# Two range checks on ScalarE instead of VectorE, and more unread products on TensorE, in a gated-recurrence and feed-forward kernel

## Chip, cores and metric

The kernel runs on one core of one Trainium2 chip. The metric is the device time of one execution in microseconds; three runs of the kernel before gave 734.25, 734.54 and 737.98 us, median 734.54 us.

## What is computed

The reference has two parts. The first is a recurrence with a complex gate per channel (4 batches, 8 heads, 768 steps, 48 channels); its result is the input of the second, a feed-forward block over 3072 tokens.

```python
# q, k, v, a_re, a_im: (B=4, H=8, S=768, D=48) float32
mag = np.sqrt(a_re * a_re + a_im * a_im)
scale = np.minimum(mag, 0.999) / (mag + 1e-06)
a_re_n, a_im_n = (a_re * scale, a_im * scale)
for t in range(S):
    S_re, S_im = a[t] * S (complex) + k[t] v[t]^T
    y[:, :, t] = q[t] . S_re
# x: y as (3072, 384); w_in (384, 2048), w_out (2048, 384), float64 in memory
h = x @ w_in
sp = np.maximum(h, 0.0) + np.log1p(np.exp(-np.abs(h)))
g = h * erf(sp)
out = g @ w_out
```

a_re lies between 0.85 and 0.95, a_im is normal with deviation 0.1.

## The kernel before

The kernel goes through 12 units of 256 steps; each unit has two chunks of 128. It has a fast way, valid where the data stay within some bounds, and a slow general way. The fast way is always run, collects six sums that say whether the data were within the bounds, and at the end one branch decides whether the general way has to follow. Two of the bounds matter here: the gate's angle has to be at most 45 degrees (`off`), and no weight may be tiny (`zeros`), since the weights are turned from float64 words into float32 by integer operations. The parts that are touched, with cuts marked:

```python
WARM = (12, 9, 8, 4, 6)
...
    for t, x in ((off, 0.0), (large, 0.0), (zeros, 1.0)):
        nc.vector.memset(t, x)
...
    def act(func, **kw):                      # loads a table where the function needs another set
        sets = [nm for nm, fs in TABLES.items() if func in fs]
        if not sets:
            nc.scalar.activation(func=func, **kw)
            return
        if T.get("table") != sets[0]:
            T["table"] = sets[0]
            in_order(nc.scalar.preload_act_table_set(sets[0]))
        in_order(nc.scalar.activation(func=func, **kw))
...
        def seek(words, i):                   # the weights' check: least absolute high word
            hi = words.bitcast(FP).rearrange("p (n w) -> p n w", w=2)[:, :, 1]
            nc.vector.tensor_reduce(out=zeros[:, i:i + 1], in_=hi, axis=mybir.AxisListType.X, op=OP.min,
                                    apply_absolute_value=True)
...                                           # begin and end: weights into float32, on ScalarE and VectorE
            ins = nc.scalar.mul(out=b, in_=lo, mul=2.0**-52)
            ins = nc.vector.tensor_scalar(out=a, in0=hi, scalar1=0x07FFFFFF, scalar2=3, ...)
            nc.vector.scalar_tensor_tensor(out=u, in0=hi, scalar=0xC0000000, in1=a, ...)
            nc.vector.tensor_scalar(out=a, in0=u, scalar1=0xFF800000, ...)
            nc.vector.tensor_tensor(out=b, in0=b, in1=a, op=OP.mult)
            nc.vector.tensor_tensor(out=f, in0=f, in1=b, op=OP.add)
        def again():                          # the weights are read once more, for the check alone
            pool, tag = ((zp, "z"), (yp, "yy"))[i % 2]
            T["raw", i] = pool.tile([P, N], I64, tag=tag, name="again")
            nc.sync.dma_start(out=split(T["raw", i]), in_=src)
        def look():
            seek(T["raw", i], i)
...
    def g_mag(u, cc=ALL):
        act(out=s, in_=ar, func=AF.Square, accum_out=large[:, i:i + 1])
        act(out=y, in_=ai, func=AF.Square)
        nc.vector.tensor_tensor(out=s, in0=s, in1=y, op=OP.add)

    def g_tan(u, cc=ALL):                     # tangent of the gate's angle, and its check
        ar, ai = gate(u, cc)
        th = g_("th", u, cc)
        act(out=th, in_=ar, func=AF.Ln)
        act(out=th, in_=th, func=AF.Exp, scale=-1.0)
        nc.vector.tensor_tensor(out=th, in0=th, in1=ai, op=OP.mult)
        i = u * C + cc[0]
        nc.vector.tensor_reduce(out=off[:, i:i + 1], in_=th, axis=mybir.AxisListType.XY, op=OP.max,
                                apply_absolute_value=True)

    def g_log(u, cc=ALL):                     # logarithm of the magnitude: Ln, Exp, Ln, then lr
...
    def warm(n, t):                           # products whose result nobody reads
        ps = ps_o.tile([P, DM], FP, tag="o", name="unread")
        for _ in range(n):
            tc.keep_in_program_order(nc.tensor.matmul(out=ps[:, 0:P], lhsT=t[:, 0:P], rhs=t[:, 0:P], start=True, stop=True))
...
    warm(WARM[0], cold)
    load_gates(0); ...                        # and the first q, k, v and weights
    for c in range(C):
        g_tan(0, one[c])
        g_mag(0, one[c])
        warm(WARM[1 + c], T["th", 0][:, c])
    g_log(0, c0)
    g_total(0, 0)                             # sum over lr, on TensorE
    ...
    g_angle(0, 0)                             # sum over th, on TensorE
    ...
    warm(WARM[3], T["th", 0][:, 1])
    g_sin(0, c0)
    for f in first[:2]: f()                   # k and q of the first chunk, turned (kt, qt)
    g_angle(0, 1)
    warm(WARM[4], T["th", 0][:, 1])
    g_sin(0, c1)
    ...
    load_gates(1)
    ...
    g_log(0, c1)
    g_total(0, 1)
    g_decay(0, 1)
    plan = list(zip(WHEN["a00"][2:], first[2:])) + ...   # all further steps with a place in the order
...
        nc.vector.tensor_scalar(out=off, in0=off, scalar1=-1.0, scalar2=0.0, op0=OP.add, op1=OP.max)
        nc.vector.tensor_scalar(out=zeros, in0=zeros, scalar1=4e-5, scalar2=None, op0=OP.is_lt)
```

Each engine works through its own instructions in a fixed order; this order follows from the plan and from a scheduler, so a change in one place can move instructions elsewhere. The weights' check reads each piece of the weights a second time, in the middle of the kernel, into buffers (`z`, `yy`) that the feed-forward part uses too; the gates' buffers (`ar`, `ai`) are single, so the next unit's gates are loaded when the last reader of the present ones is done.

Of the kernel before, what the change touches and what calls it, by code (L numbers as in the profile page):

```python
# [15 lines left out]
AF = mybir.ActivationFunctionType  # L16
OP = mybir.AluOpType
# [11 lines left out]
CAP = 0.999  # L29

# [52 lines left out]

WARM = (12, 9, 8, 4, 6)

# [510 lines left out]
def quotient_path(  # L598
# [19 lines left out]
    nc = tc.nc  # L618
# [6 lines left out]
    C = 2  # L625
# [47 lines left out]
    spans, off, large, exps, inverse, zeros = seen  # L673
    for t, x in ((off, 0.0), (large, 0.0), (zeros, 1.0)):
        nc.vector.memset(t, x)

# [22 lines left out]
    def act(func, **kw):  # L699
# [8 lines that stand above are left out]
# [38 lines left out]
    def narrow(i, dst, src, home):  # L746
# [6 lines left out]
        def seek(words, i):  # L753
            hi = words.bitcast(FP).rearrange("p (n w) -> p n w", w=2)[:, :, 1]
            nc.vector.tensor_reduce(out=zeros[:, i:i + 1], in_=hi, axis=mybir.AxisListType.X, op=OP.min,  # L755
                                    apply_absolute_value=True)

# [107 lines left out]
    def g_mag(u, cc=ALL):  # L865
# [7 lines left out]
        nc.vector.tensor_tensor(out=s, in0=s, in1=y, op=OP.add)  # L873

    def g_tan(u, cc=ALL):
        ar, ai = gate(u, cc)
        th = g_("th", u, cc)
        act(out=th, in_=ar, func=AF.Ln)
        act(out=th, in_=th, func=AF.Exp, scale=-1.0)
        nc.vector.tensor_tensor(out=th, in0=th, in1=ai, op=OP.mult)  # L880
        i = u * C + cc[0]
        nc.vector.tensor_reduce(out=off[:, i:i + 1], in_=th, axis=mybir.AxisListType.XY, op=OP.max,
                                apply_absolute_value=True)

# [378 lines left out]
    g_total(0, 1)  # L1263
    g_decay(0, 1)

    plan = list(zip(WHEN["a00"][2:], first[2:])) + list(zip(WHEN["a01"], chunk(0, 1)))
    plan += [(0.60, partial(load_qkv, 1))] + [(0.605, wt[j][0]) for j in (6, 7)]
    plan += [(WHEN["n"][j - 1], wt[j][1]) for j in range(2, 16)]
# [9 lines left out]
    for c, b in enumerate((E0, E1)):  # L1278
        plan += [(b, partial(f, 1, one[c])) for f in (g_tan, g_mag, g_log)] + [(b + 0.03, partial(g_total, 1, c))]
    plan += [(dec, partial(g_decay, 1, c)) for c in range(C)] + [(S1 + 0.001, partial(load_gates, 2))]  # L1280
# [4 lines left out]
    for u in range(NU):  # L1285
# [5 lines left out]
        if u > 1:  # L1291
            mag, log, turn, angle, decay, sin, get = WHEN["gate"].get(
                u, [u + x for x in WHEN["gr"]])
            plan += [(mag, partial(g_mag, u)), (log, partial(g_tan, u)), (log, partial(g_log, u))]
            plan += [(turn, partial(g_turn, u)), (sin, partial(g_sin, u))]
            plan += at(angle, angle + (0.35 if u > 3 else 0.05), [partial(g_angle, u, c) for c in range(C)])
            plan += at(decay, decay + 0.03, [partial(f, u, c) for c in range(C) for f in (g_total, g_decay)])
            plan += [(get, partial(load_gates, u + 1))]
# [9 lines left out]
    def check():  # L1308

        n = len(seen)  # L1310
        sums = const.tile([P, n], FP, name="sums")

        nc.vector.tensor_scalar(out=off, in0=off, scalar1=-1.0, scalar2=0.0, op0=OP.add, op1=OP.max)
        nc.vector.tensor_scalar(out=zeros, in0=zeros, scalar1=4e-5, scalar2=None, op0=OP.is_lt)
        for i, t in enumerate(seen):
# [64 lines left out]
```

## Time and profile before

| | value |
|---|---|
| time, median of 3 | 734.54 us |
| span of the profiled run, instructions | 732.5 us, 12574 |
| TensorE products / weight loads busy | 705.8 us (96%) / 601.7 us (82%) |
| vector engine busy | 599.9 us (82%) |
| ScalarE busy, of it table loads | 568.7 us (78%), 75 loads, 96.2 us |
| reductions of the weights' check (vector engine) | 14 of 128x768: 13.2 us; 4 of 128x384: 2.2 us |
| reductions of the gates' check (vector engine) | 10 of 128x768: 9.5 us; 4 of 128x384: 2.2 us |
| unread products (records; two records are one product) | 24 on `cold`: 5.0 us; 54 on `th`: 6.8 us |

In the page, PE is TensorE's product, PEld its loading of the stationary operand, DVE the vector engine, ACT ScalarE. Each line of a group has a line of the program, engine, operation, what is written and read, shapes and count, then busy time and mean duration, then the idle time of the engine just before and who ended it. The products overlap in a pipeline, so busy TensorE is not TensorE at its peak. The granted clock is a share of the full clock.

### The profile page before, as it was taken

The page shows a single profiled execution, that of the slowest core. Times are in us where ns is not written, and L with a number is a line of the kernel's source. Part 1 is how long each engine was busy: PE and PEld are TensorE (multiplying, and loading weights), DVE is VectorE, ACT ScalarE, POOL GpSimd, SP SyncE. Part 2 cuts the span into 40 slices and gives each one's busy share as a digit, 9 for nine tenths or more (in the row PEclk, how much of TensorE's full clock was granted, in tenths as well). Part 3 has the DMA queues.
Part 4 walks back from the last instruction along what each step waited for, and adds up shares of the span by engine and source line. Part 5 has one row for each costly group of instructions (what it writes and reads, how often), then busy time and mean ns, then how long its engine had stood idle before and what let it go on. Part 6 is the DMA issues. An engine that isn't in the chain of part 4 may idle for free.

```text
span 732.5 us, 12574 instructions
## 1 busy us (share of the span) xinstructions
PE 705.8 (96%) x5018; PEld 601.7 (82%) x5018; DVE 599.9 (82%) x1031; ACT 568.7 (78%) x751; POOL 1.1 (0%) x8
## 2 busy tenths in 40 slices
PE   8798899899999999999999999999999999999996
PEld 6676688676777669899898898899899899899985
DVE  6899999677869599979989979888978877876554
ACT  8976677998988998979788688788588488557760
POOL 0000000000000000000000000000000000000000
PEclk9899999999999999999999999999999999999999
DMA  9973666120303020441521422422321400200000
GB/s 218 235 173 87 155 176 163 28 43 22 56 12 56 22 63 15 100 96 40 124 55 44 119 55 60 105 56 55 109 80 40 130 1 12 98 2 21 1 23 27
DMA packets 156012, 54.50 MB, mean 74 GB/s; under 512 B 142612, under 2 KB 145704, under 8 KB 155944
## 3 DMA queue, kind: packets, MB, share of 16 engines
q1 hardware_dynamic: 153864, 53.22, 30.9%
q8 instruction: 41, 0.67, 0.4%
q10 hardware_dynamic: 2080, 0.39, 0.3%
q14 instruction: 27, 0.22, 0.1%
HBM read 48.82 MB, written 4.75 MB: 73 GB/s over the span
## 4 chain that ended last, share of the span: by engine, by line
PE 59%; DVE 17%; ACT 15%; DMA 4%; issue 2%; SPq 1%; ACTq 0%; DVEq 0%
PE hps L1055 20%; PE ops L1153 14%; PE ops L1115 6%; PE tr L975 4%; PE y L1035 4%; PE sc L986 4%; ACT yy L707 3%; PE kv L998 3%; ACT L706 3%; ACT z L707 2%; DVE z L1083 2%; DVE e L1085 2%; DVE yy L1084 2%; DVE h L1086 2%; DMA again<-in_moe_w_in_dram 2%
## 5 line engine op out<-in xcount | busy, mean ns | idle before, releaser
L1055 PE MATMUL hps<-xT,w_in_sb 128*128 128x256 f32 x1152 | 272.1, 381 | 3.8 <-DVE w_in_sb L784 1.8
L1055 PEld LDWEIGHTS hps<-xT,w_in_sb 128*128 128x128 f32 x1152 | 212.5, 190 | 37.3 <-issue 3.4
L706 ACT ACT_TABLE_LOAD x75 | 96.2, 1283 | 3.3 <-issue 2.1
L1057 ACT COPY h<-hps 128x512 f32<-128x512 f32 x96 | 55.4, 581 | 49.7 <-PE hps L1055 47.3
L1083 DVE TENSOR_TENSOR z<-z,yy 128x512 f32<-128x512 f32 x96 | 62.7, 685 | 33.2 <-ACT e L707 32.7
L707 ACT ACTIVATE e<-z 128x512 f32<-128x512 f32 x96 | 57.3, 626 | 36.8 <-DVE h L1086 36.4
L1115 PE MATMUL ops<-w_out_sb,h 128*128 128x384 f32 x224 | 78.0, 490 | 0.1
L1153 PE MATMUL ops<-w_out_sb,h 128*128 128x192 f32 x384 | 70.3, 326 | 0.0
L1153 PEld LDWEIGHTS ops<-w_out_sb,h 128*128 128x128 f32 x384 | 63.5, 190 | 1.4
L1085 DVE TENSOR_TENSOR e<-e,yy 128x512 f32<-128x512 f32 x96 | 62.6, 684 | 0.2
L1084 DVE SCALAR_TENSOR_TENSOR yy<-z,yy 128x512 f32<-128x512 f32 x96 | 62.5, 684 | 0.2
L1086 DVE SCALAR_TENSOR_TENSOR h<-e,h 128x512 f32<-128x512 f32 x96 | 62.5, 684 | 0.1
L1115 PEld LDWEIGHTS ops<-w_out_sb,h 128*128 128x128 f32 x224 | 41.2, 190 | 24.9 <-DVE h L1086 1.2
L707 ACT ACTIVATE z<-h 128x2048 f32<-128x2048 f32 x24 | 45.9, 1913 | 9.0 <-DVE seen L755 4.7
L986 PEld LDWEIGHTS sc<-qT,kT 96*128 96x128 f32 x384 | 49.3, 197 | 3.8 <-ACT qT L978 0.4
L986 PE MATMUL sc<-qT,kT 96*128 96x128 f32 x384 | 51.4, 282 | 0.3 <-ACT qT L978 0.3
L1035 PE MATMUL y<-A,v 128*32 128x128 f32 x768 | 48.9, 284 | 1.2 <-DVE A L989 1.1
L1153 PE MATMUL ops<-T,S 128*128 128x192 f32 x256 | 47.3, 327 | 0.0
L707 ACT ACTIVATE yy<-z 128x2048 f32<-128x2048 f32 x24 | 45.9, 1914 | 0.4
L707 ACT ACTIVATE z<-z 128x2048 f32<-128x2048 f32 x24 | 45.9, 1913 | 0.3
L707 ACT ACTIVATE yy<-yy 128x2048 f32<-128x2048 f32 x24 | 45.9, 1912 | 0.3
L1035 PEld LDWEIGHTS y<-A,v 128*32 128x32 f32 x768 | 34.9, 110 | 10.9 <-issue 4.7
(105 smaller groups left out, 1094.7 us busy)
## 6 DMA issues: line engine op xcount, KB each, us to landing
raw<-in_moe_w_in_dram SPq DMA_DIRECT2D x8, 768.0 KB, 8.3
raw<-in_moe_w_out_dram SPq DMA_DIRECT2D x8, 768.0 KB
again<-in_moe_w_in_dram SPq DMA_DIRECT2D x8, 768.0 KB, 6.6
ar<-in_a_re_dram SPq DMA_DIRECT2D x24, 192.0 KB, 3.3
k<-in_k_dram SPq DMA_DIRECT2D x24, 192.0 KB, 4.2
q<-in_q_dram SPq DMA_DIRECT2D x24, 192.0 KB, 3.5
v<-in_v_dram SPq DMA_DIRECT2D x48, 96.0 KB, 2.4
out_dram<-o SPq DMA_DIRECT2D x24, 192.0 KB, 1.9
```

The lines of the kernel that those rows point to most:

```text
L706: in_order(nc.scalar.preload_act_table_set(sets[0]))
L707: in_order(nc.scalar.activation(func=func, **kw))
L986: nc.tensor.matmul(out=ps[:, j, :], lhsT=st["k", g][0:D2, j, :], rhs=st["q", g][0:D2, j, :], start=True, stop=True)
L1035: nc.tensor.matmul(out=ps[b * QUAD:(b + 1) * QUAD, i, :], lhsT=lhsT, rhs=rhs, start=start, stop=stop)
L1055: nc.tensor.matmul(out=ps[:, e, :], lhsT=w_in_sb[:, kd, f0:f0 + P], rhs=T["xT", u][:, kd, :], start=(kd == 0), stop=(kd == KD - 1))
L1057: nc.scalar.copy(out=T["h", u, sl][:, i:i + 2, :], in_=ps)
L1083: nc.vector.tensor_tensor(out=z, in0=z, in1=y, op=OP.mult)
L1084: nc.vector.scalar_tensor_tensor(out=y, in0=z, scalar=-2.0, in1=y, op0=OP.add, op1=OP.mult)
L1085: nc.vector.tensor_tensor(out=e, in0=e, in1=y, op=OP.mult)
L1086: nc.vector.scalar_tensor_tensor(out=h, in0=e, scalar=1.0 / RT2, in1=h, op0=OP.add, op1=OP.mult)
L1115: nc.tensor.matmul(out=ps, lhsT=lhsT, rhs=w_out_sb[:, i, :], start=i == HALF, stop=i == KF - 1)
L1153: ins = nc.tensor.matmul(out=ps, lhsT=a(sl)[:, i], rhs=b(sl, i), start=sl == 0 and i == 0, stop=sl == NSL - 1 and i == HALF - 1)
```

## The change

The two checks leave the vector engine's reductions. The gates' check becomes |ai| - ar on ScalarE (Abs), the vector engine (subtraction) and ScalarE again (Relu with a small bias, summed over the row), in a step of its own, `g_off`. The weights' check squares the high words on ScalarE and sums an exponential with a steep negative factor: only tiny words leave anything in the sum. With this the two operations that prepared `off` and `zeros` at the end fall away. On TensorE there are more products that nobody reads: two groups between the first sums and the first transpositions grow from 4 to 8 and from 6 to 13, and a new group of 5 gets a place among the first transpositions. They are there so that TensorE is not left idle in its pauses.

```diff
--- before.py
+++ after.py
@@ -28,6 +28,7 @@
 }
 CAP = 0.999
 
+LEAST = 2.0**-30
 
 
 LIMITS = (1e13, 0.0, 1e15, 1e18, 1e8, 1e-6)
@@ -83,7 +84,7 @@
  'al': [[11.0, 11.39], [11.319, 11.75]]}
 
 
-WARM = (12, 9, 8, 4, 6)
+WARM = (12, 9, 8, 8, 13, 5)
 
 @with_exitstack
 def product_path(
@@ -671,8 +672,8 @@
     widths = (NU * C, NU * C, NU * C, NU * NSL, NU * NSL, 18)
     seen = [const.tile([P, n], FP, name=f"seen{i}") for i, n in enumerate(widths)]
     spans, off, large, exps, inverse, zeros = seen
-    for t, x in ((off, 0.0), (large, 0.0), (zeros, 1.0)):
-        nc.vector.memset(t, x)
+    for t in (off, large, zeros):
+        nc.vector.memset(t, 0.0)
 
     w_in_sb = const.tile([P, KD, FF], FP, name="w_in_sb")
     w_out_sb = const.tile([P, KF, DM], FP, name="w_out_sb")
@@ -752,8 +753,8 @@
 
         def seek(words, i):
             hi = words.bitcast(FP).rearrange("p (n w) -> p n w", w=2)[:, :, 1]
-            nc.vector.tensor_reduce(out=zeros[:, i:i + 1], in_=hi, axis=mybir.AxisListType.X, op=OP.min,
-                                    apply_absolute_value=True)
+            act(out=hi, in_=hi, func=AF.Square)
+            act(out=hi, in_=hi, func=AF.Exp, scale=-1e10, accum_out=zeros[:, i:i + 1])
 
         split = lambda t: t.rearrange("p (k n) -> p k n", k=k_)
 
@@ -872,15 +873,21 @@
         act(out=y, in_=ai, func=AF.Square)
         nc.vector.tensor_tensor(out=s, in0=s, in1=y, op=OP.add)
 
+    def g_off(u, cc=ALL):
+
+        ar, ai = gate(u, cc)
+        m = T["y"][:, cc[0]:cc[1]]
+        i = u * C + cc[0]
+        act(out=m, in_=ai, func=AF.Abs)
+        nc.vector.tensor_tensor(out=m, in0=m, in1=ar, op=OP.subtract)
+        act(out=m, in_=m, func=AF.Relu, bias=LEAST, accum_out=off[:, i:i + 1])
+
     def g_tan(u, cc=ALL):
         ar, ai = gate(u, cc)
         th = g_("th", u, cc)
         act(out=th, in_=ar, func=AF.Ln)
         act(out=th, in_=th, func=AF.Exp, scale=-1.0)
         nc.vector.tensor_tensor(out=th, in0=th, in1=ai, op=OP.mult)
-        i = u * C + cc[0]
-        nc.vector.tensor_reduce(out=off[:, i:i + 1], in_=th, axis=mybir.AxisListType.XY, op=OP.max,
-                                apply_absolute_value=True)
 
     def g_log(u, cc=ALL):
         s, y = T["s"][:, cc[0]:cc[1]], T["y"][:, cc[0]:cc[1]]
@@ -1262,8 +1269,11 @@
     g_log(0, c1)
     g_total(0, 1)
     g_decay(0, 1)
+    for cc in one:
+        g_off(0, cc)
 
     plan = list(zip(WHEN["a00"][2:], first[2:])) + list(zip(WHEN["a01"], chunk(0, 1)))
+    plan += [(0.41, partial(warm, WARM[5], T["th", 0][:, 1]))]
     plan += [(0.60, partial(load_qkv, 1))] + [(0.605, wt[j][0]) for j in (6, 7)]
     plan += [(WHEN["n"][j - 1], wt[j][1]) for j in range(2, 16)]
     plan += [(WHEN["n"][5] + 0.001 * j, wt[j][0]) for j in (8, 9)] + [(WHEN["n"][j - 1] + 0.001, wt[j + 2][0]) for j in range(8, 14)]
@@ -1276,7 +1286,7 @@
         plan += [(u, wt[i][2]), (look, wt[i][3])]
     E0, E1, dec, T0, T1, S0, S1 = WHEN["g1"]
     for c, b in enumerate((E0, E1)):
-        plan += [(b, partial(f, 1, one[c])) for f in (g_tan, g_mag, g_log)] + [(b + 0.03, partial(g_total, 1, c))]
+        plan += [(b, partial(f, 1, one[c])) for f in (g_tan, g_mag, g_log, g_off)] + [(b + 0.03, partial(g_total, 1, c))]
     plan += [(dec, partial(g_decay, 1, c)) for c in range(C)] + [(S1 + 0.001, partial(load_gates, 2))]
     for c, (t, b) in enumerate(((T0, S0), (T1, S1))):
         plan += [(t, partial(g_turn, 1, one[c])), (t + 0.005, partial(g_angle, 1, c)), (b, partial(g_sin, 1, one[c]))]
@@ -1291,7 +1301,7 @@
         if u > 1:
             mag, log, turn, angle, decay, sin, get = WHEN["gate"].get(
                 u, [u + x for x in WHEN["gr"]])
-            plan += [(mag, partial(g_mag, u)), (log, partial(g_tan, u)), (log, partial(g_log, u))]
+            plan += [(mag, partial(g_mag, u)), (mag, partial(g_off, u)), (log, partial(g_tan, u)), (log, partial(g_log, u))]
             plan += [(turn, partial(g_turn, u)), (sin, partial(g_sin, u))]
             plan += at(angle, angle + (0.35 if u > 3 else 0.05), [partial(g_angle, u, c) for c in range(C)])
             plan += at(decay, decay + 0.03, [partial(f, u, c) for c in range(C) for f in (g_total, g_decay)])
@@ -1309,9 +1319,6 @@
 
         n = len(seen)
         sums = const.tile([P, n], FP, name="sums")
-
-        nc.vector.tensor_scalar(out=off, in0=off, scalar1=-1.0, scalar2=0.0, op0=OP.add, op1=OP.max)
-        nc.vector.tensor_scalar(out=zeros, in0=zeros, scalar1=4e-5, scalar2=None, op0=OP.is_lt)
         for i, t in enumerate(seen):
             nc.vector.tensor_reduce(out=sums[:, i:i + 1], in_=t, axis=mybir.AxisListType.X, op=OP.add)
         ps = ps_b.tile([P, n], FP, tag="b", name="all")
```

## Prediction

> **What bounds the kernel now.** I read the busy times first, then five long stretches, then what TensorE waits for, and last the timeline around the stretch that the change touches. The first part of the page (engine, busy us, share, instructions):
>
> ```profile
> PE 705.8 (96%) x5018; PEld 601.7 (82%) x5018; DVE 599.9 (82%) x1031; ACT 568.7 (78%) x751; POOL 1.1 (0%) x8
> ```
>
> TensorE leads, but an average hides stages. The busy time by stretch (from:to and length, then PE, PEld, DVE, ACT, POOL, granted clock, DMA share, GB/s):
>
> ```profile
> 0.00:146.00 146.00, 127.72 (x993) 106.66 (x994) 126.63 (x207) 114.61 (x192) 1.09 (x8) 0.96 0.68 155
> 146.00:293.00 147.00, 146.32 (x865) 107.37 (x864) 118.45 (x205) 130.21 (x154) 0.00 (x0) 1.00 0.18 36
> 293.00:622.00 329.00, 327.36 (x2504) 294.48 (x2503) 284.55 (x493) 263.58 (x340) 0.00 (x0) 1.00 0.30 71
> ```
>
> From 146 to 622 us TensorE stands still for 0.68 + 1.64 = 2.3 us. Nothing taken off another engine there can bring more than that; work put on another engine can only cost. In the first 146 us TensorE is idle for 18.3 us and waits for the others. The waits of TensorE (line, releaser, us in total, times, longest):
>
> ```profile
> PE tr L975 <- DVE kt L967: 4.5, 6, 1.8
> PE tr L975 <- DVE qt L967: 2.2, 1, 2.2
> PE hps L1055 <- DVE w_in_sb L784: 1.8, 1, 1.8
> PE tr L975 <- ACT qT L978: 1.7, 1, 1.7
> ```
>
> Most of this lies before 146 us: the transpositions wait for the vector engine, which from 36.6 to 73.2 us is busy 99% (36.09 of 36.60), mostly with the conversion of the weights. The clock in two-us steps shows the second loss (same columns as above):
>
> ```profile
> 22.00:24.00 2.00, 1.29 (x6) 1.02 (x7) 1.90 (x4) 2.00 (x6) 0.00 (x0) 0.65 0.92 151
> 24.00:26.00 2.00, 1.60 (x6) 0.86 (x5) 1.04 (x2) 1.72 (x5) 0.00 (x0) 0.50 0.79 199
> 26.00:28.00 2.00, 2.00 (x9) 1.70 (x8) 1.11 (x2) 1.46 (x5) 0.00 (x0) 0.50 1.03 382
> 28.00:30.00 2.00, 2.00 (x16) 2.00 (x14) 1.51 (x3) 2.00 (x7) 0.00 (x0) 0.64 1.05 402
> ```
>
> After pauses of 2.15 and 1.66 us before the transpositions the granted clock halves for some 7 us. At full clock the same work would be 1.29 x 0.35 + 1.60 x 0.50 + 2.00 x 0.50 + 2.00 x 0.36 = 3.0 us shorter. In the timeline (start, length):
>
> ```profile
> 22.71 1.08 PE L975 MATMUL tr<-ident,kt 128*96 128x128 f32 x4 [1.66 <-ACT qT L978]
> 25.09 1.65 PE L927 MATMUL sum<-lr,triu 128*128 128x384 f32 x2 [0.40 <-DVE lr L891]
> 26.54 3.33 PE L986 MATMUL sc<-qT,kT 96*128 96x128 f32 x16
> ```
>
> The same groups take 0.64, 0.88 and 2.05 us elsewhere (at 19.97, 10.77 and 35.72 us).
>
> **What the Trainium skill says.** "TensorE: Matmul & The Clock Gate", part 1 on the clock gate: the clock is halved after an idle window of about 3.4 us and restored by a busy one. The trace agrees in kind: 0.50 granted after two pauses that together are 3.8 us, and 1.00 again from 30 us. "ScalarE: Activation LUTs", on the cost of a table load: about 1283 ns, then one element per cycle, with neighbours overlapping by some 93 ns. The trace has 1283 ns for 75 loads, and activations of 384 and 768 elements that last 0.51 and 0.84 us but follow each other every 0.41 and 0.75 us. The same page, on table sets: cheap functions such as Relu and Abs are in every set, so the gate check needs no load; Exp does. "VectorE: DVE Perf Modes", on the tiers: tensor_reduce and fp32 tensor_tensor both run at the basic rate; the trace has 947 ns for the one and 0.95 us for the other, at 128x768.
>
> **The change part by part.**
>
> Unread products. Three groups grow: by 4 (before the second sum of angles), by 7 (before the first transpositions) and by 5 (new, after the first eight transpositions). Seventeen such products took 4.28 us, so 0.25 us each: 1.0, 1.75 and 1.25 us. The pauses they fall into are 1.27, 2.15 and 1.66 us, so all fit. I expect the clock to stay at 1.0 and 3.0 us of TensorE time to be saved. On the chain lies the sum over lr (0.77 us), then the scores' 1.28 us, in part.
>
> Gate check. Fourteen reductions (9.5 + 2.2 = 11.7 us of the vector engine) go, fourteen subtractions of the same size come: 10 x 0.95 + 4 x 0.55 = 11.7 us, no difference. New on ScalarE: Abs, Relu and the reading of the sum: 10 x (2 x 0.75 + 0.09) + 4 x (2 x 0.41 + 0.09) = 15.9 + 3.6 = 19.5 us.
>
> Weight check. Eighteen reductions go from the vector engine: 13.2 + 2.2 = 15.4 us. ScalarE gets Square and Exp instead. The 128x768 multiply at L769, which also reads every second word, starts its successor after 0.81 us, so 14 x (2 x 0.81 + 0.09) + 4 x (2 x 0.45 + 0.09) = 23.9 + 4.0 = 27.9 us (0.45 for the half size is my estimate from the 0.41 us of a dense one). The order of instructions shows 77 table loads for 75: 2.6 us, both around the last look, between two pairs of Gelu.
>
> Sum: ScalarE 568.7 + 50.0 = about 619 us (84%), the vector engine 584.5 us (80%), TensorE's necessary work +4.0 us in idle time.
>
> Order. In the new order the vector engine makes kr, qr, kt and qt of the second chunk before the masked scores of the first, and converts the third piece of w_in some 5 us earlier; I count about 1.0 us less idle time for it between 24 and 29 us (2.3 us now, against my walk through the new order: some 1.3). Against this ScalarE, which is busy 31.6 of the first 36.6 us, gets an Abs (0.41) and a Relu (0.51) ahead of the second lr, so lr comes about 0.5 us later. Net for the vector-bound stretch: -1.0 us. Near 125 us ScalarE is itself the chain (its operations follow each other without a break from 119 to 143 us while TensorE pauses for 3.4 us); unit 3's gate check adds 1.6 us there, and one square of unit 4 (0.75 us) leaves: +0.85 us. So at 146 us the two kernels stand about level, the changed one at -0.2 us.
>
> Middle. From 293 to 622 us ScalarE gets all looks (27.9 + 2.6 us) and some six gate checks (9.5 us): 263.6 + 40 = 304 of 329 us, 92% where it is 80% now. It has 29.4 us of waiting for TensorE's products, 18.0 for the vector engine and 15.0 for y in that stretch, so the work fits into gaps in the sum. But a copy of products out of PSUM that comes behind a look is up to 1.7 us late, and the look moves from the vector engine to just ahead of the exponentials of the sums, for which a 0.95 us reduction becomes 1.7 us of two activations. Most of these delays meet the second PSUM buffer (12 records of products last 2.6 us). I let 1.5 us of all come through as TensorE idle time. The vector engine's 15.4 us bring nothing here, since TensorE stands still for 1.6 us only. End: unchanged.
>
> 734.5 - 0.2 + 1.5 = 735.8 us.
>
> **The rivals.** (1) ScalarE becomes the bound of the middle. For it: 92%, with table loads and in-order waits for the re-read weights in between; between 220 and 293 us it is at 91% already. Against it: TensorE is fed from two streams, and ScalarE's largest waits today are for TensorE. It would give 741 to 747 us. (2) The middle hides everything and only the beginning counts, with the clock's 3 us mostly on the chain: 731 to 733 us. For it: TensorE idles for 18 us before 146 us, and the second chunk's kt comes some 2 us earlier. Against it: from 36 us on the vector engine sets the pace, and it doesn't care for the clock. (3) The next unit's gates come late. The check reads ar and ai once more, so the loads of unit 1, which are issued from 18.2 us on now, stand behind three pieces of w_in in the new order, and the logarithm of ar stands on ScalarE ahead of the second chunk's kT copy. If they land after 31 us, ScalarE waits and the gain at the start turns into +2 to +3 us: 738 us. Against it: the pieces of w_in move at 380 to 400 GB/s and should be through by 26 us.
>
> **Range and chances.** Start and chain near 125 us: -3 to +3. Middle: 0 to +6. I take 731.5 to 742.0 us. Two per cent is 14.7 us; only rival 1 in a severe form comes near, and nothing gives that much the other way: faster 0.01, within 0.96, slower 0.03. That it is a little slower I hold for somewhat likelier than a little faster.
>
> **What would show it.** Right: granted clock 1.0 from 10 to 32 us, the sum at about 25 us in 0.9 us; ScalarE's busy time near 619 us, the vector engine's near 585; TensorE idle by one to three us more between 146 and 622 us, with releasers on ScalarE; first products into w_in at about 41 us as now. Wrong: a clock of 0.5 all the same; ScalarE waiting for ar or ai of unit 1 near 30 us; more than 5 us of idle TensorE in the middle (rival 1), or none there and a start two us earlier (rival 2).

## The result, and the profile after

| kernel | median | lowest to highest | runs |
|---|---|---|---|
| before | 734.79 us | 734.25 to 737.98 us | 4 |
| changed | 744.98 us | 744.02 to 745.80 us | 4 |

The ratio of the means is 1.0129, with a 95% interval of 1.0097 to 1.0161: the changed kernel is 9.5 us slower by the means and 10.2 us by the medians. The prediction said 735.8 us, with a range up to 742.0; the measured median is 9.2 us above the one and 3.0 us above the other.

The first part of the page of the changed kernel (engine, busy us, share, instructions), and the first line of its chain that ended last:

```profile
PE 709.7 (96%) x5050; PEld 605.4 (82%) x5050; DVE 585.9 (79%) x1011; ACT 617.6 (83%) x849; POOL 1.1 (0%) x8
```

```profile
PE 43%; ACT 27%; DVE 19%; DMA 7%; issue 2%; SPq 0%
```

The sums of work came out as worked out: ScalarE 617.6 us (619 predicted), the vector engine 585.9 (584.5), TensorE 3.9 us more (4.0). What is new is the chain: ScalarE holds 27% of it, where the kernel before has 15%, and DMA 7% for 4%; TensorE has fallen from 59% to 43%. The extra time isn't TensorE's own.

The same stretches as in the prediction, of the changed kernel (from:to and length, then busy time of PE, PEld, DVE, ACT, POOL, granted clock, DMA share, GB/s):

```profile
0.00:146.00 146.00, 131.20 (x1012) 109.11 (x1013) 120.61 (x197) 116.81 (x202) 1.08 (x8) 0.98 0.68 155
146.00:293.00 147.00, 142.80 (x851) 103.98 (x850) 118.74 (x204) 134.40 (x167) 0.00 (x0) 1.00 0.18 36
293.00:622.00 329.00, 322.30 (x2467) 290.33 (x2466) 269.87 (x472) 286.44 (x385) 0.00 (x0) 1.00 0.29 68
```

From 146 to 622 us TensorE now stands still for 4.2 + 6.7 = 10.9 us, where it was 2.3, all at full clock. These 8.6 us are not all new: part of the 4.2 is a pause that lay ahead of 146 us before (see the gates' check below). The waits of TensorE (line, releaser, us in total, times, longest):

```profile
PE hps L1062 <- DVE w_in_sb L785: 4.6, 2, 3.5
PE tr L982 <- DVE kt L974: 3.9, 5, 1.2
PE kv L1005 <- ACT pr L708: 3.8, 6, 1.2
PE tr L982 <- ACT qT L985: 1.8, 1, 1.8
```

Two waits have grown: for the last piece of converted weights (1.8 to 4.6 us) and for pr, ScalarE's exponentials of the sums (it was 0.6 us in 2 waits before). The granted clock where the kernel before had 0.65, 0.50, 0.50 and 0.64:

```profile
22.00:24.00 2.00, 0.25 (x3) 0.05 (x1) 1.90 (x3) 1.99 (x7) 0.00 (x0) 1.00 1.00 365
24.00:26.00 2.00, 1.66 (x9) 1.03 (x10) 1.46 (x3) 1.83 (x5) 0.00 (x0) 1.00 1.05 399
26.00:28.00 2.00, 1.85 (x19) 1.53 (x17) 0.67 (x2) 2.00 (x7) 0.00 (x0) 1.00 0.35 116
28.00:30.00 2.00, 1.32 (x11) 1.32 (x12) 2.00 (x5) 1.69 (x5) 0.00 (x0) 1.00 0.93 188
```

and, from its timeline (start, length), the groups shown of before:

```profile
25.51 0.91 PE L934 MATMUL sum<-lr,triu 128*128 128x384 f32 x2
26.63 0.37 SPq L727 DMA_DIRECT2D ar<-in_a_re_dram  x1
28.68 2.05 PE L993 MATMUL sc<-qT,kT 96*128 96x128 f32 x16 [0.83 <-ACT qT L985]
```

The sum takes 0.91 us instead of 1.65 and the scores 2.05 instead of 3.33: the unread products do what they are for. But the scores start at 28.68, 2.1 us later than before (26.54), and the load of unit 1's gates is issued at 26.6 us, where it was 18.2.

To say where the time comes in, I worked out of each trace when the same share of TensorE's necessary products (all but those that nobody reads, each counted with its usual spacing, the median distance to the next start) is done. Behind the kernel before the changed one is by +1.0 us at 42 us, +4.1 at 104, +4.5 at 125, +1.3 at 145, +6.1 at 205, +4.8 at 300, +7.1 at 490, and +9.1 at the end. I call this the lag. It is of one profiled run per kernel, and an estimate that is good to about half a microsecond; where two kernels do the products in another order, as around 145 us, it is rougher.

### The profile page after: what moved, and what is told of

It reads as the page before. It is cut to its first block, busy times and chain, and to the rows that moved or that the text cites. A ratio compares the mean times of both kernels' runs of the same rounds, so it can differ in the third digit from the quotient of the medians.

```text
span 742.6 us, 12738 instructions
## 1 busy us (share of the span) xinstructions
PE 709.7 (96%) x5050; PEld 605.4 (82%) x5050; DVE 585.9 (79%) x1011; ACT 617.6 (83%) x849; POOL 1.1 (0%) x8
## 4 chain that ended last, share of the span: by engine, by line
PE 43%; ACT 27%; DVE 19%; DMA 7%; issue 2%; SPq 0%
PE hps L1062 14%; PE ops L1122 8%; PE ops L1160 7%; ACT L707 4%; ACT z L708 4%; ACT yy L708 4%; DVE yy L1091 3%; DVE z L1090 3%; PE sc L993 3%; DVE e L1092 3%; PE y L1042 3%; PE kv L1005 3%; PE tr L982 2%; ACT pr L708 2%; DMA again<-in_moe_w_in_dram 2%
## 5 line engine op out<-in xcount | busy, mean ns | idle before, releaser
L993 PEld LDWEIGHTS sc<-qT,kT 96*128 96x128 f32 x384 | 47.3, 192 | 3.9 <-ACT qT L985 1.3
```

What stands on the lines that cost most here:

```text
L993: nc.tensor.matmul(out=ps[:, j, :], lhsT=st["k", g][0:D2, j, :], rhs=st["q", g][0:D2, j, :], start=True, stop=True)
```

## The experiments

All ratios are of means, to runs of the kernel before on the same chip, in the same series, whose medians were 735.9 to 736.8 us; one per cent is 7.4 us. The difference of two ratios is uncertain by some 2 to 3 us. Two executions far outside the rest, one of the kernel before (2115 us, in the series of e9 to e12) and one of e12 (1882 us), are left out of the ratios.

| run | ratio | 95% interval | median us |
|---|---|---|---|
| e1 unread products only | 0.9955 | 0.9941 to 0.9970 | 733.32 |
| e2 both checks, no new products | 1.0185 | 1.0142 to 1.0228 | 748.66 |
| e3 gates' check only | 1.0097 | 1.0061 to 1.0133 | 742.79 |
| e4 weights' check only | 1.0115 | 1.0077 to 1.0154 | 743.48 |
| e5 as e3, from unit 1 on | 1.0060 | 1.0037 to 1.0084 | 740.12 |
| e6 as e3, from unit 4 on | 1.0021 | 1.0004 to 1.0038 | 737.49 |
| e7 as e4, look 0.08 units later | 1.0081 | 1.0056 to 1.0106 | 741.79 |
| e9 as e3, unit 0 reads the sum | 1.0102 | 1.0058 to 1.0145 | 743.46 |
| e10 as e4, look at resident weights | 1.0014 | 0.9988 to 1.0040 | 736.27 |
| e11 no gates' check at all | 1.0019 | 0.9999 to 1.0039 | 737.99 |
| e12 as e1, 16 more products | 0.9951 | 0.9934 to 0.9967 | 732.50 |
| e13 as e1, with e4's check | 1.0056 | 1.0034 to 1.0077 | 738.92 |
| e14 as e13, nothing to wait for | 0.9978 | 0.9963 to 0.9992 | 734.68 |
| e16 as e1, no gates' check at all | 0.9984 | 0.9960 to 1.0007 | 735.55 |
| e17 as e1, with e3's check | 1.0106 | 1.0071 to 1.0140 | 742.84 |

e8, e15 and e18 left so much of a check out that its bound was exceeded, and the general way was run after the fast one (some 2290 us). Only the part of their traces before that is read.

### The parts one by one

e1 takes the unread products alone:

```diff
-WARM = (12, 9, 8, 4, 6)
+WARM = (12, 9, 8, 8, 13, 5)
+    plan += [(0.41, partial(warm, WARM[5], T["th", 0][:, 1]))]
```

> Only the unread products are changed (groups of 8, 13 and 5 in place of 4, 6 and none); both checks stay on the vector engine, and every engine but TensorE has the very order of the kernel before. Theory A (the loss comes from the checks; the clock's 3 us lie partly on the chain): 732 to 733.5 us, granted clock 1.0 from 14 to 30 us. Rival B (from 36 us on the vector engine sets the pace, so the clock is worth nothing at the end): 734 to 735 us. Rival C (the unread products themselves are in the way): 736 us or more.

Measured: 0.9955, that is 3.3 us faster, and a narrower spread: 731.2 to 734.2 us in 22 runs, where the kernel before has 732.5 to 740.8 in 27. The order on the other engines doesn't change, so this is the products' doing. The two profiled executions differ by less, 734.0 against 734.5 us: by the lag e1 is 3.1 us ahead at 85 us, 0.6 at 145 and 0.1 at 196, and it ends level. What the products save in that pair is waited away later, as rival B has it. The mean granted clock was 0.981 to 0.993 over the 27 runs of the kernel before (0.991 in the profiled one) and 0.993 to 0.997 over e1's 22; so the 3.3 us come, as far as these figures show, from executions in which the clock was low for longer than in the profiled one.

e2 takes both checks without the products (the change with WARM left as before):

> Both checks as in the changed kernel, the unread products as before; ScalarE, the vector engine and the DMA queue have the very order of the changed kernel. Theory A: the whole loss is here, 745 to 748 us, and the difference to the changed kernel (0 to 3 us) is what the unread products are worth beside the checks. Rival C: 735 to 740 us, the products being the loss.

Measured: 1.0185. The products seem to be worth something with the checks too (1.0185 against 1.0129), though the two intervals just overlap.

e3 has only g_off in place of the vector engine's maximum over th, e4 only Square and Exp in place of its minimum over the words:

```diff
# e3
+        act(out=m, in_=ai, func=AF.Abs)
+        nc.vector.tensor_tensor(out=m, in0=m, in1=ar, op=OP.subtract)
+        act(out=m, in_=m, func=AF.Relu, bias=LEAST, accum_out=off[:, i:i + 1])
-        nc.vector.tensor_reduce(out=off[:, i:i + 1], in_=th, axis=mybir.AxisListType.XY, op=OP.max, ...)
# e4
-            nc.vector.tensor_reduce(out=zeros[:, i:i + 1], in_=hi, axis=mybir.AxisListType.X, op=OP.min, ...)
+            act(out=hi, in_=hi, func=AF.Square)
+            act(out=hi, in_=hi, func=AF.Exp, scale=-1e10, accum_out=zeros[:, i:i + 1])
```

> Only the gates' check goes to ScalarE (19.5 us of ScalarE by my sum, the vector engine level); weights' check and unread products as before. Theory A1 (loss in proportion to ScalarE's added time, 19.5 of 50 us): 738 to 739 us. Theory A2 (the gates' check is the loss, by what it delays in the first 220 us, where the changed kernel has already lost 6 us): 740 to 743 us. Theory A3 (the weights' check is the loss): 734 to 736 us.

> Only the weights' check goes to ScalarE (30.5 us, from 300 us on; 15.4 us less for the vector engine); gates' check and unread products as before, and the order is that of the kernel before up to about 290 us. Theory A1: 740 to 741 us. Theory A2: 735 to 738 us, with the lag growing after 300 us alone. Theory A3: 743 us or more.

Measured: 1.0097 and 1.0115, so 7.1 and 8.5 us. Both checks cost, about the same each; with e1's gain the parts add up to 12.3 us, against 9.5 by the ratio of the whole, which is no difference within what is measured. The prediction had +0.5 us (lr later) and +0.85 us (near 125 us) for the first, and 1.5 us for both in the middle.

### The gates' check

e5 and e6 leave the check of the first unit, or of the first four, with the vector engine:

```diff
+        if u < ONVEC:      # 1 in e5, 4 in e6
+            return         # in g_off; g_tan keeps the maximum for these units
```

> The gates' check goes to ScalarE from unit 1 on; unit 0 keeps its reduction on the vector engine, so nothing but the tangent and the magnitude reads the gates of unit 0 and the loads of unit 1's gates go out at about 18 us again. All units on ScalarE cost 7 us. Theory D (the loss begins with these late loads, the rival of my prediction): 3 to 5 us over the kernel before, with the second chunk's lr of unit 1 near 40 us and not 44. Theory E (ScalarE's added time in the first 200 us, wherever it is): 6 to 7 us, since unit 0 has only 1.9 of the 8.7 us of the first five units.

> The gates' check goes to ScalarE from unit 4 on (8 of 12 units, 12.7 of 19.5 us by my sum); units 0 to 3 keep the reduction. Theory E and D alike (the loss belongs to the first 200 us, where ScalarE stands on the chain): 0 to 2 us over the kernel before. Theory F (every piece of work on ScalarE costs, in proportion): 4 to 5 us.

Measured: 1.0060 and 1.0021. Of 7.1 us, unit 0 carries 2.7, units 1 to 3 carry 2.9, and units 4 to 11, which have most of ScalarE's added work, only 1.5. How the 5.6 us are shared between unit 0 and units 1 to 3 is uncertain by as much as the shares themselves; that units 4 to 11 carry little is clear. The cost lies in the first 200 us.

One cause there could be the late load of unit 1's gates, since the check reads ar and ai once more (my third rival). e9 lets the check of unit 0 read another tile, so that the loads go out early:

```diff
+        if u == 0:
+            ar = ai = T["lr", 0][:, cc[0]:cc[1]]
```

> As e3 (the gates' check by the scalar engine, everything else as before, 1.0097), but the check of unit 0 reads the sum of its gates twice, in place of their two inputs, so that unit 1's gates can be loaded into those inputs as early as in the kernel before (18.2 us, not 26.6). The engines do the same amount of work; what the check says of unit 0 is left out. e5 (unit 0 left to the vector engine) was 2.7 us faster than e3. Theory D, unit 0's share comes from the late loads of unit 1's gates: about 4 us above the kernel before, as e5. Theory E, it comes from the scalar engine's own time ahead of the logarithms: about 7 us above it, as e3.

Measured: 1.0102, though the trace has the load back at 18.29 us. That is nearer to e3 (1.0097) than to e5 (1.0060) and speaks against the late loads as the cause, but it doesn't settle it: e9's interval takes in e5's value, and its profile, of its fastest run, ends with a lag of 6.3 us, where e5's has 5.5 and e3's 8.7.

Where time goes can be followed in the timelines of the vector engine and ScalarE during the conversion of the weights. In e1 (start, length):

```profile
43.40 0.92 ACT L769 ACTIVATE raw<-raw 128x768 f32<-128x768 uint32 x1
45.01 0.96 DVE L783 TENSOR_TENSOR raw<-raw,word 128x768 f32<-128x768 f32 x1
...
64.87 0.94 DVE L784 TENSOR_TENSOR w_in_sb<-w_in_sb,raw 128x768 f32<-128x768 f32 x1
...
65.87 4.34 PE L1055 MATMUL hps<-xT,w_in_sb 128*128 128x256 f32 x12 [1.85 <-DVE w_in_sb L784]
```

and in the changed kernel:

```profile
43.68 0.53 ACT L703 ACTIVATE y<-ai 128x384 f32<-128x384 f32 x1 [0.22 <-DVE lr L898]
...
45.23 0.51 ACT L703 ACTIVATE y<-y 128x384 f32<-128x384 f32 x1
...
48.49 0.91 ACT L770 ACTIVATE raw<-raw 128x768 f32<-128x768 uint32 x1
49.43 0.97 DVE L784 TENSOR_TENSOR raw<-raw,word 128x768 f32<-128x768 f32 x1 [2.66 <-ACT raw L770]
...
65.65 0.95 DVE L882 TENSOR_TENSOR y<-y,ar 128x768 f32<-128x768 f32 x1
...
71.18 0.94 DVE L785 TENSOR_TENSOR w_in_sb<-w_in_sb,raw 128x768 f32<-128x768 f32 x1
...
72.18 4.21 PE L1062 MATMUL hps<-xT,w_in_sb 128*128 128x256 f32 x9 [3.51 <-DVE w_in_sb L785]
```

For each piece of weights the vector engine has five operations, and the last two of them need the result of a ScalarE multiply (raw). By 48 us ScalarE has had four pairs of Abs and Relu in its queue, those of units 0 and 1 (the last ones at 43.68 and 45.23 us), about 0.9 us a pair by the prediction's figure; and unit 1's logarithms, which e1 has behind it by 37 us, last until 42 us here. The multiply comes 5 us later, at 48.49, and the vector engine stands still for 2.66 us in the very stretch where it was busy 99%. Unit 2's subtraction (65.65 us) then goes ahead of another piece. The last piece is ready at 72.1 us, where e1 has it at 65.8. TensorE waits 3.51 us for it instead of 1.85, and after that wait the granted clock is 0.50 from 72 to 76 us. This is the chain that the trace shows up to 104 us, where the lag is 4.1 us. That the late multiply is what costs the time is not shown by it; e18 below has a multiply as late and ends without loss.

Later, too, TensorE waits where it didn't. The stretch from 146 to 205 us of e1, e17 (e1 and the gates' check), e13 (e1 and the weights' check) and the changed kernel, in this order:

```profile
146.00:205.00 59.00, 59.00 (x341) 41.91 (x340) 42.96 (x74) 51.24 (x60) 0.00 (x0) 1.00 0.22 41
```

```profile
146.00:205.00 59.00, 55.16 (x299) 38.05 (x301) 50.09 (x85) 53.58 (x69) 0.00 (x0) 1.00 0.21 38
```

```profile
146.00:205.00 59.00, 59.00 (x339) 41.54 (x338) 42.29 (x73) 52.52 (x61) 0.00 (x0) 1.00 0.21 41
```

```profile
146.00:205.00 59.00, 55.15 (x294) 38.34 (x292) 50.28 (x85) 53.55 (x71) 0.00 (x0) 1.00 0.21 38
```

TensorE's idle time goes from none to 3.84 us wherever the gates' check is on ScalarE in the early units (e5 and e9 have 3.9 too; e6, from unit 4 on, has 1.7), and ScalarE is 91% busy there. In the changed kernel it is made mostly of four short waits: 1.2 us for kt, 1.0 for h, 0.8 for kT, 0.6 for pr. But this is for the most part an old pause in a new place. From 125 to 146 us, in e1 and then in e17:

```profile
125.00:146.00 21.00, 17.43 (x79) 14.22 (x78) 14.24 (x22) 19.02 (x29) 0.00 (x0) 0.92 0.25 40
```

```profile
125.00:146.00 21.00, 20.68 (x144) 16.93 (x143) 11.85 (x17) 20.89 (x29) 0.00 (x0) 1.00 0.39 85
```

e1 is idle for 3.6 us there and e17 for 0.3, so that from 125 to 205 us the two come to 3.6 and 4.2 us. e15, which has the gates' check on the vector engine, shows the same shift (0.4 us of idle time, then 2.9). And by the lag e17 is behind e1 by 2.7 us at 42 us, 4.8 at 75, 5.1 at 104, 5.5 at 125, 5.6 at 205 and 5.8 at 622: what the gates' check costs has been lost by about 104 us, half of it before 42 us, that is before the late multiply.

e11 and e16 leave the check out altogether, without and with the products of e1, to see what the vector engine's relief is worth:

```diff
-        nc.vector.tensor_reduce(out=off[:, i:i + 1], in_=th, axis=mybir.AxisListType.XY, op=OP.max, ...)
```

> The kernel before with the check of the gates left out altogether (neither the vector engine's maximum nor anything in its place; what it says is left out). The vector engine does 11.7 us less. Theory V, the vector engine sets the pace of the first 80 us, as the prediction had it, so that its relief is worth time there: 2 to 4 us faster than the kernel before. Theory S, the scalar engine sets it and a relief of the vector engine is worth nothing: 0 to 1 us faster.

> e1 with the gates' check left out altogether (11.7 us less for the vector engine, nothing in its place). e11's trace, beside that of the kernel before, gained 1.5 us between 42 and 104 us and lost them to a longer fall of the granted clock before and after. If the vector engine's relief is worth that much: 0.992 to 0.9935. If nothing: 0.9955, as e1.

Measured: 1.0019 and 0.9984. 11.7 us less for the vector engine make nothing faster; e16 is even 2.1 us slower than e1, with intervals that just overlap. What changes besides is only the order in which the engines take their work. So of any cost here some 2 us may be order, and e15 (below) shows more. e11's own profile lost 3.9 us to the clock by 42 us (below).

e17 and e18 set the whole check and half of its scalar work on e1:

```diff
# e18
-        act(out=m, in_=ai, func=AF.Abs)
-        nc.vector.tensor_tensor(out=m, in0=m, in1=ar, op=OP.subtract)
-        act(out=m, in_=m, func=AF.Relu, bias=LEAST, accum_out=off[:, i:i + 1])
+        act(out=m, in_=ar, func=AF.Relu, bias=LEAST, accum_out=off[:, i:i + 1])
```

> e1 (unread products, 0.9955) with the gates' check by the scalar engine (e3, 1.0097). If the two add up: about 1.005. The base for e18.

> e17 with the absolute value and the subtraction left out: only the half-wave with its sum is left, read straight from the gates' real part (so it says nothing of 45 degrees). The scalar engine's added work is halved, and nothing of the check waits for the vector engine. Theory S, the cost goes with the scalar engine's work: half of e17's share, about 1.000. Theory O, it is the wait for the subtraction between the two halves: 0.996 to 0.998. Theory R, it is the changed order: 1.004 to 1.006, as e17.

Measured: e17 is 1.0106, 11 us above e1 (its runs lie in two groups, near 740 and near 744.6 us and above; the profile is of the first, where the difference is 5.8 us by the lag). e18's time is that of the general way; in its trace the lag, up to 710 us, is 1.0 us less than e1's and 6.8 less than e17's. Half of ScalarE's work and no subtraction cost nothing that the trace shows, although the multiply of weights comes as late as with the whole check (at 47.69 us; the vector engine waits 2.83 us for it). TensorE's wait for the last piece is 1.9 us, and from 146 to 205 us it is idle for 0.75. Up to 42 us e18 loses almost as much against e1 as e17 does (2.3 and 2.7 us); after that it makes the loss good, and e17 doesn't. e18 differs from e17 in three things at once: half of ScalarE's work is gone, the vector engine's subtractions are gone (11.7 us, in e1 the reductions of the same length), and the instructions of all three engines stand in another order from about 24 us on. So the cost is tied to the check as a whole in the first units; whether it is the second scalar operation, the subtraction on the vector engine or the order was not told apart, and the cause of this part stays open.

### The weights' check

e7 moves the look behind the exponentials that it stands ahead of:

```diff
-            plan += [(u, wt[i][2]), (u + 0.22, wt[i][3])]
+            plan += [(u, wt[i][2]), (u + 0.30, wt[i][3])]
```

> As the kernel with the weights' check alone on ScalarE, but the looks of units 6 to 11 stand 0.08 of a unit later in the plan, so that most of them come after the exponentials of the sums (pr) and just ahead of the next softplus. Theory H (the look holds up pr, and with it the scaled k and TensorE, which waited for pr four times): 1 to 4 us over the kernel before, where the earlier place cost 8 us. Theory I (it is ScalarE's time as such, or the wait for the re-read weights, which now holds up the softplus): 6 us or more.

Measured: 1.0081 against e4's 1.0115, intervals overlapping. Its ScalarE still waits 8.9 us for the second transfers (6.2 and 2.7), so the place alone settles little.

e8 halves the work of the look: the square with its sum is left, the exponential is left out.

```diff
-            act(out=hi, in_=hi, func=AF.Square)
-            act(out=hi, in_=hi, func=AF.Exp, scale=-1e10, accum_out=zeros[:, i:i + 1])
+            act(out=hi, in_=hi, func=AF.Square, accum_out=zeros[:, i:i + 1])
```

> As the kernel with the weights' check alone on ScalarE, at the old place, but the look is one Square with its sum; the Exp is left out, so the sum says nothing of tiny weights. ScalarE's addition falls from 30.5 us to some 14.5 us (no table loads either). Theory I (time as such): 4 us over the kernel before, half of 8. Theory H (the in-order place ahead of pr, behind the wait for the re-read weights): 5 to 7 us, since the wait for the landing stays.

Measured, from its trace: the lag grows by 3.4 us between 300 us and the end of the fast way, where e4's profile has 5.8. ScalarE waits 10.9 us for the transfers in it, no less than in e4.

That wait is what e10 takes away. The look squares the resident weights, and the second transfer is left out:

```diff
-            act(out=hi, in_=hi, func=AF.Square)
+            act(out=hi, in_=home_of, func=AF.Square, bias=1.0)
-            nc.sync.dma_start(out=split(T["raw", i]), in_=src)     # in again()
```

> As e4 (the weights' check by the scalar engine, 1.0115), but the square and the exponential read the resident weights, to which 1 is added; the second transfer of the weights into a buffer of their own is left out, so that nothing is to be waited for at the look but the engine's turn. What is computed says nothing of tiny weights. Theory W, the look costs mostly because the scalar engine, which works in order, waits at it for the second transfer (4.9 and 0.8 us of such waits in the profile after): 2 to 4 us above the kernel before. Theory S, it costs the scalar engine's own 30 us, which push back the copies and exponentials that TensorE waits for: 5 to 8 us above it.

Measured: 1.0014, where e4 has 1.0115. The same 30 us of ScalarE's work cost 1.0 us (-0.9 to +2.9) instead of 8.5. The middle stretch of e4 and of e10:

```profile
293.00:622.00 329.00, 322.54 (x2462) 289.29 (x2461) 266.29 (x465) 280.76 (x371) 0.00 (x0) 1.00 0.29 69
```

```profile
293.00:622.00 329.00, 327.57 (x2500) 294.03 (x2499) 272.23 (x477) 283.87 (x378) 0.00 (x0) 1.00 0.20 38
```

ScalarE is busier in e10 (283.9 us against 280.8), and TensorE's idle time falls from 6.5 to 1.4 us. The busy share of ScalarE is not what holds TensorE up.

e10 leaves out the transfer along with the wait. e13 to e15, on the steadier e1, part the two: e13 is e1 with e4's check; e14 looks at the resident weights, while half of each transfer still goes into a part of the buffer that nobody reads; e15 leaves the look with the vector engine, over the resident weights, without a transfer.

```diff
# e14
+            nc.sync.dma_start(out=split(T["raw", i][:, 0:N // 2]), in_=src[:, :, 0:n // 2])
+            act(out=hi, in_=home_of, func=AF.Square, bias=1.0)      # hi: the other half
# e15
+            nc.vector.tensor_reduce(out=zeros[:, i:i + 1], in_=home_of, op=OP.min, ...)   # no transfer
```

> e1 (unread products, 0.9955) with the weights' check by the scalar engine (e4, 1.0115). If the two add up: 0.9955 + 0.0115 = about 1.007. The base for e14.

> e13 with the square and the exponential on the resident weights plus 1; half of each second transfer is kept, into a part of its buffer that nobody reads, so the scalar engine has the same work but no transfer to wait for. What is computed says nothing of tiny weights. Theory W, the cost is the scalar engine's in-order wait for the transfer: 0.995 to 0.998, as e1. Theory T, it is the traffic: halfway between, about 1.001. Theory S, it is the scalar engine's own time: 1.004 to 1.007, as e13.

> e1 with the vector engine's minimum taken over the resident weights and the second transfer left out (says nothing of the words as they lie in memory). If neither the transfer nor the vector engine's wait for it costs anything: as e1, 0.9955. If leaving out the transfer is itself worth time, that share of e10's gain was not the scalar engine's wait: 0.991 to 0.993.

Measured: e13 1.0056, e14 0.9978. The look costs 7.4 us over e1 with the wait and 1.7 without. What ScalarE waited for in e13 and in e14, as far as the look is concerned (line, releaser, us in total, times, longest):

```profile
ACT again L702 <- DMA again<-in_moe_w_out_dram: 6.8, 5, 1.9
...
ACT again L702 <- DMA again<-in_moe_w_in_dram: 1.7, 3, 1.3
```

```profile
ACT again L702 <- DVE yy L1087: 1.9, 2, 1.5
```

and the middle stretch of e13, then of e14:

```profile
293.00:622.00 329.00, 324.17 (x2482) 290.88 (x2481) 268.36 (x467) 280.87 (x374) 0.00 (x0) 1.00 0.29 69
```

```profile
293.00:622.00 329.00, 326.80 (x2495) 293.03 (x2495) 271.55 (x476) 281.98 (x380) 0.00 (x0) 1.00 0.25 54
```

TensorE is idle for 4.8 us with the wait and 2.2 without, and e1 itself has 2.0. On the same chip, e13 and e14 are 5.7 us apart. e15's time is that of the general way; in the same stretch of its trace TensorE is idle for 1.3 us, so the traffic left out is worth at most 0.7 us of idle time there. But e15 is no clean partner of e1: with nothing to wait for, its looks moved forward to between 18 and 327 us (in e1 they lie between 315 and 633), eight of them to between 18 and 87 us, and by the lag its fast way is 3.6 us behind e1, all of it lost before 300 us. Whether that is the vector engine's added work in its busiest stretch or the order was not told apart. The in-order wait for the transfer, together with the look, is the greater part of the weights' check. It isn't all: e8 keeps the wait, halves the work, and costs less (3.4 against 5.8 us by the traces). It would fit that wait and work add to one delay ahead of a copy that TensorE needs, and that a small delay is swallowed where a large one isn't; no run shows this by itself. One reserve stays: from about 300 us on e10 and e14 also stand in another order than e4 and e13, which can be worth 2 us (e16) or more (e15); the differences of 7.4 and 5.7 us are larger, and two pairs of kernels agree.

### A better version

e12 adds to e1 sixteen more unread products in three later pauses:

```diff
+    plan += [(t, partial(warm, n, triu)) for t, n in ((1.28, 6), (1.36, 4), (2.9, 6))]
```

> e1 (the unread products alone, 0.9955) with 16 more unread products on TensorE in three later pauses (6, 4 and 6, between 64 and 145 us, where e1's granted clock still fell to 0.69 to 0.89). The order on the other engines is that of the kernel before. If those falls cost time as the first one did: up to 2 us below e1, 0.993 to 0.9955. If the products cost as much as they save there: as e1.

Measured: 0.9951, no better than e1 (0.9955) within what is measured. In its profile the clock stays at 1.0 up to 140 us, where e1's fell to 0.69 at 68 to 72 us, but both meet at 160 us: what is won at one pause is waited away at the next. e1 is the version to keep: 3.3 us faster than the kernel before by the means, without either check on ScalarE.

## Why the prediction was wrong

**Unread products: right on the clock, lucky on the gain.** The clock stays at 1.0 from 10 to 32 us, the sum takes 0.91 us, all fit their pauses. Alone they are worth 3.3 us (0.9955), near the 3.0 of TensorE time worked out. But these are not the same 3 us: in the two profiles the time saved is gone by 196 us, and the gain in the means comes, as far as the clocks show, from executions in which the clock was low for longer. That the figures meet is then chance. What the prediction didn't know is that 3.0 us was one run's figure. The slow phase after 22 us has no fixed length. In e11's profile (clock in the third column from the end):

```profile
24.00:28.00 4.00, 3.62 (x13) 2.57 (x12) 2.17 (x4) 3.19 (x10) 0.00 (x0) 0.50 0.87 274
28.00:32.00 4.00, 4.00 (x25) 4.00 (x23) 2.62 (x4) 3.97 (x10) 0.00 (x0) 0.50 0.90 332
32.00:36.00 4.00, 4.00 (x45) 3.34 (x45) 3.31 (x8) 0.96 (x3) 0.00 (x0) 0.50 1.00 178
36.00:40.00 4.00, 3.75 (x29) 3.62 (x28) 1.48 (x5) 2.67 (x7) 0.00 (x0) 0.75 1.02 200
```

and in that of the kernel before:

```profile
24.00:28.00 4.00, 3.60 (x13) 2.55 (x12) 2.15 (x4) 3.18 (x9) 0.00 (x0) 0.50 0.91 291
28.00:32.00 4.00, 4.00 (x59) 3.89 (x57) 3.41 (x5) 3.97 (x10) 0.00 (x0) 0.82 0.87 315
```

The same thirteen products in 24 to 28 us are followed by full clock from about 30 us in the kernel before and by half clock till 38 us in e11. In the traces' records of the clock the phase lasts 6.83 us in the profile before, 17.07 in e11's and 20.48 in e8's: 2, 5 and 6 times 3.41 us. The Trainium skill, "TensorE: Matmul & The Clock Gate", part 1, says that the window which decides is free-running; phases of whole windows fit that. Two things don't fit what the prediction took from that page. TensorE was not idle for a whole window before the fall: in the 3.41 us up to 22.60 us it was busy for 1.08. And one busy window did not restore the clock: in e11 TensorE is busy for 8.00 of the 8 us from 28 to 36 us, at 0.50. Why the phase is so much longer in some runs stays open. The same part puts the penalty of a warm-up below 1% of a typical span; e8's profile, which has the same order as before up to 300 us, lost 5.4 us or 0.7% more than the profile before in this one phase.

**Sums of work: right**, within 1.4 us on each engine. They were the easy part, and they didn't decide the time.

**Order, "Net for the vector-bound stretch: -1.0 us": the first step that failed.** (Its own two terms, 1.0 us less idle time and lr 0.5 us later, give -0.5.) Measured at 104 us: 4.1 us behind the kernel before; and the gates' check alone, e17 against e1, costs 5.1 us by then. The prediction looked for ScalarE's Abs and Relu only ahead of lr (0.5 us), and took the vector engine for the one that sets the pace from 36 to 73 us. That engine is fed: two of its five operations on each piece need a ScalarE multiply, which came 5 us late and left it idle for 2.66 us. A busy share of 99% said that the vector engine had no slack, not that nothing else could stop it. e16 adds that relieving it brings nothing at the end. What is shown is that the check in units 0 to 3 costs this time (e3 against e6); which part of it, the scalar work, the subtraction or the order that follows, stays open (e18). "So at 146 us the two kernels stand about level" came close by the lag (+1.3 us at 145 us) through luck: e3, without the products, shows the same dip (1.6), because products that are done earlier than before fill a pause there and are missing later; at 205 us the lag is 6.1.

**Middle, "I let 1.5 us of all come through": the second.** Measured: 6.7 us of idle TensorE from 293 to 622 us, 5.1 more than before. The prediction weighed ScalarE's sum against its gaps (92% said; 87% measured, four of the 18 looks coming after 622 us) and the length of a look (1.7 us) against the second PSUM buffer. It named the in-order wait for the re-read weights, but only as a word in rival 1, with no size. The runs give it: with that wait 7.4 us, without 1.7, close to the 1.5 that the prediction had for looks and gate checks together. Its estimate fits a look that never waits.

**End unchanged:** by the lag 622 us and the end are within 2 us of each other; nothing is added there.

**Rivals.** The first had the time (741 to 747 us), and its sign, more than 5 us of idle TensorE in the middle, came true (6.7); but its reason was wrong in part: ScalarE isn't the bound by its share (e10), it is late by its waits. The second named the clock's gain, but not what the checks would take. The third came true as an event (26.6 us); e9 speaks against it as a cause without settling it.

## What to carry to other kernels

Before moving a small operation to an engine with room, look at what it will wait for there. ScalarE works in order and also empties PSUM, so that its waits for a transfer reached TensorE here: about 30 us of added work cost 1.7 us without such a wait and 7.4 us with it. An engine at 99% can still be stopped by the one that feeds it, as the 2.66 us of idle vector engine show; whether such a stop costs time at the end has to be measured, since e18 had one as long (2.83 us) and had lost nothing at the end. Compare stretches of time with care: a pause that moves across the border of a stretch looks like a new one. And where the clock falls in the pauses of a chain, a few products that nobody reads are worth trying alone, apart from whatever else the change brings, with enough runs to see the spread.

## What was not expected

- The unread products narrow the spread more than they lower the median: 3.0 us between lowest and highest of 22 runs, against 8.2 us of 27.
- The length of the slow-clock phase differs from run to run: 6.8 us in the profile before and 20.5 in e8's, with the same instructions on TensorE up to there, and 17.1 in e11's, each a whole multiple of 3.41 us.
- Taking 11.7 us of work off the vector engine made the kernel 2 us slower (e16 against e1, at the edge of what is measured): the order that follows from it may be worth as much as many a change.
